# Two transformer layers on one core: gate values kept in SBUF for a batched gelu, DMA moves ordered by readiness with the broadcast split in four, paced block work, and two-bank score slots at the layer boundary

## The chip, the cores and the metric

The kernel runs on one core of one Trainium2 chip. The metric is the device time of one execution in microseconds (us). A quoted time is the median of several executions; a ratio is the mean time of one kernel's fast runs over the mean time of the other's fast runs of the same rounds, so it is not quite the ratio of the medians. Waits, busy times and stretches come from one profiled execution of each kernel, so a difference of spans need not equal that of the medians to the microsecond.

Five engines matter here. TensorE ("PE" in the profile, "PEld" for its weight loads) does all matrix products. ScalarE ("ACT") does exponentials and gelu. VectorE ("DVE") empties PSUM, does the statistics of the layer norms and takes over a part of the exponentials. GpSimd ("POOL") does a few products. The sync engine ("SP") only issues DMA.

## The reference, cut to what matters

One sequence of 2048 tokens, width 512, 32 heads of 16, a GEGLU hidden width of 1792. Two layers with the same weights:

```python
def _A_ref(x, wqkv, wo):                       # attention, 32 heads of 16
    qkv = (x @ wqkv).reshape(B, S, 3, H, Dh).transpose(2, 0, 3, 1, 4)
    q, k, v = qkv[0], qkv[1], qkv[2]
    scores = jnp.einsum("bhqd,bhkd->bhqk", q, k) * (Dh ** -0.5)
    p = jax.nn.softmax(scores, axis=-1)
    o = jnp.einsum("bhqk,bhkd->bhqd", p, v)
    return o.transpose(0, 2, 1, 3).reshape(B, S, D) @ wo

def _B_ref(x, w_gate, w_up, w_down):
    return (gelu_tanh(x @ w_gate) * (x @ w_up)) @ w_down

x = x + _A_ref(layernorm(x), wqkv, wo)
x = x + _B_ref(layernorm(x), w_gate, w_up, w_down)
x = x + _A_ref(layernorm(x), wqkv, wo)         # second layer, same weights
x = x + _B_ref(layernorm(x), w_gate, w_up, w_down)
```

## The kernel before

**A static order, made by a model.** The Python program does not loop over tiles in a fixed nest. It holds a small event model of the core, asks at each step which work is ready, emits that work, and advances the model's clock. What comes out is one fixed instruction order for each engine, with semaphores where data is passed on. So the durations in the model decide the *order*, the chip decides the *times*, and an engine that meets an instruction whose data is late stands until it is there, as PE does for 2.83 us in a view below.

**Attention.** A block is 512 queries. It has 8 units (4 heads each), and a unit has 64 score tiles of 128 keys by 512 queries. Score tiles are written by PE into a "slot" of up to three PSUM banks; there are two slots (banks 0 to 2 and 3 to 5). Bank 7 accumulates probabilities times V, bank 6 is the only spare bank. ScalarE exponentiates the tiles of a slot. In groups of 12 tiles (4 slots of 3), one tile of each slot can go to VectorE instead: it writes a rough exponential as integers, and three shifted copies that PE then multiplies too refine it. A VectorE group turns four three-bank exponentials into four two-bank ones.

```python
def vector_group():                    # may the next group of 12 use VectorE?
    if pend.get(("PI", dg_no[0] % NPI)):
        return False
    late = max(0.0, sch.free["dve"] - now[0]) + sum(op[3] for j in jobs["dve"] for op in j[2])
    late += 0.6 * len(shifts)
    return late < DVE_LATE

def a_slot(entry):
    layer, u, part, tiles, dslot, end = entry
    if dslot is not None:
        if dslot % 4 == 0:
            use["d"] = (layer or u) and vector_group()
        if not use["d"]:
            dslot = None
    ...
    na = n - (dslot is not None)       # tiles of this slot that ScalarE takes
    pe(fn, ...)                        # n score matmuls into the slot's banks
    o = sch.op("act", lambda e: e.activation(PT[...], PS[:, b0:b0 + na, :], ACTF.Exp, ...), ...)
```

**The post.** When a block's eight units are done, its "post" follows: normalise, output projection, residual, layer norm, gates, gelu, up, down, residual, layer norm. The post is a Python generator of PE pieces, and the pieces are put between the exponentials of the *next* block. That is what keeps ScalarE fed. At the boundary of the layers, the second layer starts with six units split in two parts, A (48 tiles) before the fourth post of the first layer is done and B after it.

Normalising sends the reciprocals of the softmax sums through a DRAM scratch and broadcasts them over partitions. GpSimd multiplies, and half of the products are moved by DMA from ATS into AT, the stationary operand of the output projection:

```python
def dma(eng, grp, dst, src, r=(), w=(), serial=False, kb=32):   # the model's price of a move
    t = max(sch.free[eng], sch.ready(eng, r, w)) + 0.5
    wire[0] = max(t, wire[0]) + kb / 180.0
    return sch.op(eng, ..., cost=0.5, lat=wire[0] - t + 1.7)

def spread():                                          # one unit's broadcast and product
    i, g = rest.pop(0)
    slot = rb_no[0] % NRB                              # NRB = 2 buffers
    dma("sp", "rb%d" % slot, RB[:, slot, :],
        AP(RSC, (half * 16 * HB + 16 * i) * 128, [[512, 4], [0, 32], [1, 512]]),
        r=[("RSC", half)], w=[("RB", slot)], serial=True, kb=256)
    ...
    def done(o):
        if odd:
            for j in range(4):
                dma("sp", "at%d_%d" % (c % 2, j), AT[32 * j + 16:32 * j + 32, c, :],
                    ATS[32 * j:32 * j + 16, c % 2, :], ...)
        ...
        spread()
    job("pool", 1, [(lambda e: e.tensor_tensor(dst, OS[:, os_, :], RB[:, slot, :], op=ALU.mult), ...)], done)
```

A DMA is issued at the point where the program asks for it, and SP works through its moves in that order. So a move whose data is late can hold back those behind it, the weight loads among them (two runs below show it: PE waits 19.4 us for down-projection weights with this order, in e8, and 2.5 us with moves ordered by readiness, in e5).

**Gates and gelu.** The gates of the post take over the two score slots. While they run there are no exponentials, only pairs of gate tiles and gelus from PSUM:

```python
def fill():
    if gq:
        return g_slot(*gq.pop(0))      # a pair of gate tiles instead of scores
    ...
def g_slot(qb, k):
    pe(fn, xk(qb) + [("WR", s)], bks, 8 * MM)           # 8 gate matmuls, two banks
    sch.op("act", lambda e: e.activation(HT[:, 2 * k:2 * k + 2, :], PS[:, b0:b0 + 2, :],
                                         ACTF.Gelu_apprx_tanh), ...)
```

**Where a piece of the post may go.** A piece is emitted when it fits into the time until ScalarE needs the next slot, with a tolerance. The tolerance grows when the post has fallen behind a count of slots; at the last block of a layer it is unlimited:

```python
def post_tol():
    if pace["haste"]:                  # the last post of a layer
        return 99.0
    return 1.0 if slot_no[0] > pace["start"] + 12 + 2.2 * pace["n"] else 0.1
```

If PE has nothing to do, the program emits dummy matmuls ("keep-clock" matmuls, the line with fONB and fZV) meant to keep TensorE's granted clock from dropping.

## Time and profile before

| | before |
|---|---|
| device time, median of 4 | 1822.8 us (1821.11 to 1826.94) |
| mean granted TensorE clock | 0.984 |
| exponentials on ScalarE | 1408 |
| score tiles on VectorE | 956 of 4096 |
| bytes moved by DMA | 126.14 MB |

The page's first part gives each engine's busy time, its share of the span, and its instructions.

```profile
span 1823.5 us, 39987 instructions
PE 1681.1 (92%) x17053; PEld 512.5 (28%) x17053; DVE 1410.7 (77%) x2322; ACT 1530.2 (84%) x1484; POOL 216.4 (12%) x237
```

PE looks like the limit, but 271.8 us of its time are keep-clock dummies. ScalarE has 293 us of idle time, and the question is what ended each idle stretch. This is ScalarE's list of waits before: what waited, for what, the us in total, how many times, and the longest one.

```profile
ACT fPT L1067 <- PE fPS L1062: 173.1, 104, 32.3
ACT fHT L1027 <- PE fPS L1021: 69.4, 49, 32.9
ACT fXNT L540 <- PE fPS L531: 17.5, 4, 15.6
```

Exponentials (fPT) wait 173.1 us for score matmuls, 32.3 us of it in one piece. Gelus (fHT) wait 69.4 us for gate matmuls; 32.9 us of that is a single wait in the tail, the rest is a steady drip, as ScalarE's timeline of one gelu phase before shows (start, duration, engine, line, operation, in brackets the idle time before it):

```profile
1407.48 1.02 ACT L1027 ACTIVATE fHT<-fPS 128x1024 bf16<-128x1024 f32 x1 [1.35 <-PE fPS L1021]
1409.20 1.02 ACT L1027 ACTIVATE fHT<-fPS 128x1024 bf16<-128x1024 f32 x1 [0.70 <-PE fPS L1021]
1410.93 1.02 ACT L1027 ACTIVATE fHT<-fPS 128x1024 bf16<-128x1024 f32 x1 [0.70 <-PE fPS L1021]
```

A pair of gates takes PE 1.73 us and a gelu 1.02 us, so ScalarE idles 0.7 us a pair. The table loads (1.28 us each, one before and one after the phase) come on top.

PE's own list of waits before has two lines that end in a DMA:

```profile
PE fPS L554 <- DMA fAT<-fATS: 16.8, 7, 3.2
PE fPS L858 <- DMA fWR<-in_B_w_down_dram: 14.1, 10, 5.2
```

The first is the output projection, standing for the copy of ATS into AT. What such a wait does is seen in the timeline of one post's start before:

```profile
1159.14 2.41 SPq L276 DMA_DIRECT2D fAT<-fATS  x4
...
1162.88 1.86 PE L554 MATMUL fPS<-fWO,fAT 128*128 128x512 bf16 x4 [2.83 <-DMA fAT<-fATS]
...
1164.67 1.03 PE L1062 MATMUL fPS<-fQ,fKT 32*128 32x512 bf16 x6
1165.33 1.94 ACT L1067 ACTIVATE fPT<-fPS 128x1024 bf16<-128x1024 f32 x2 [4.43 <-PE fPS L1062]
...
1166.04 1.05 PE L1172 MATMUL fPS<-fPP,fVD 128*17 128x512 f16 x4
...
1168.54 1.94 ACT L1067 ACTIVATE fPT<-fPS 128x1024 bf16<-128x1024 f32 x2 [1.28 <-PE fPS L1062]
...
1170.35 0.60 PE L1062 MATMUL fPS<-fQ,fKT 32*128 32x512 bf16 x6
```

PE stands 2.83 us. ScalarE then idles 4.43 us, and 1.28 us once more three microseconds later.

Why is the copy late? The chain of waits before passes through the broadcast of the reciprocals (start, duration, what):

```profile
463.86 7.04 DMA fRB<-rscr
...
1141.20 6.85 DMA fRB<-rscr
...
1152.39 5.30 DMA fRB<-rscr
```

The model allows 256/180 + 1.7 = 3.1 us for a lone 256 KB move. The broadcast took 5 to 7 us, with two under way. The DMA view of the kernel before, cut to the 7.5 us after 463.5, shows the busy share of the core's 16 DMA engines in tenths, and what they moved:

```profile
DMA  0000011112222222222222232252222222100002
GB/s 0 0 0 0 0 22 33 66 76 87 98 109 98 98 98 98 109 98 87 109 98 98 98 120 87 109 186 98 98 109 98 98 98 87 66 22 22 0 0 33
```

While nothing but broadcasts moves, "2" is two tenths and up to three of sixteen engines, hence 3.2 to 4.8 engines, at about 100 GB/s. The Trainium skill (DMA: Bandwidth & Descriptors, section "Why a DMA increments its semaphore by 16 and not by 1") says that a move uses the largest number of engines, at most 16, that divides the slowest dimension of both access patterns. The source of the broadcast is `[[512, 4], [0, 32], [1, 512]]`; its slowest dimension is 4, so four engines, and this trace agrees with that.

Last, ScalarE's timeline before at the layer boundary, the two longest idle stretches of the program outside its start and tail:

```profile
906.86 5.71 ACT L1067 ACTIVATE fPT<-fPS 128x1536 bf16<-128x1536 f32 x5 [32.31 <-PE fPS L1062]
...
1045.57 17.52 ACT L1067 ACTIVATE fPT<-fPS 128x1024 bf16<-128x1024 f32 x19 [28.62 <-PE fPS L1062]
```

### The profile page before, as it was taken

The numbers are of one execution on the slowest core, as the hardware profiler recorded it, in microseconds if no ns is written. First come the engines' busy times: TensorE is split into PE (matmuls) and PEld (weight loads), VectorE is DVE, ScalarE is ACT, GpSimd is POOL, SyncE is SP. The second block draws the span as 40 slices with busy tenths as digits, with TensorE's granted clock in tenths as the row PEclk, the third lists the DMA queues.
The fourth block names the chain that finished last, engine by engine and source line by source line (L and its number), as shares of the span: only waits on it lengthen the run. The fifth ranks groups of instructions, "written<-read, shape, count | busy, mean of one in ns | idle before, by whom it ended". The sixth has DMA issues, their size and how long they took to land.

```text
span 1823.5 us, 39987 instructions
## 1 busy us (share of the span) xinstructions
PE 1681.1 (92%) x17053; PEld 512.5 (28%) x17053; DVE 1410.7 (77%) x2322; ACT 1530.2 (84%) x1484; POOL 216.4 (12%) x237
## 2 busy tenths in 40 slices
PE   8998989999898998999899989899989999899998
PEld 3422223222232222322332322232223222232233
DVE  4798876889868878699568598769876988768853
ACT  2699998989889998899289389889998999889931
POOL 2402010011111021010331120101010010101010
PEclk9999999999999999999999999999999999999999
DMA  5200000152022410223312500023501152023403
GB/s 151 71 2 29 2 28 26 53 156 80 28 65 80 145 54 11 58 81 99 109 47 70 168 28 3 28 60 89 158 28 36 48 163 62 28 61 110 127 21 100
DMA packets 142775, 126.14 MB, mean 69 GB/s; under 512 B 8704, under 2 KB 126208, under 8 KB 142592
## 3 DMA queue, kind: packets, MB, share of 16 engines
q1 hardware_dynamic: 138320, 115.12, 21.1%
q0 software_dynamic: 4272, 8.39, 1.7%
q8 instruction: 139, 2.28, 0.5%
q14 instruction: 44, 0.36, 0.1%
HBM read 109.84 MB, written 6.82 MB: 64 GB/s over the span
## 4 chain that ended last, share of the span: by engine, by line
ACT 38%; PE 34%; DVE 12%; DMA 11%; SPq 2%; POOL 2%; issue 1%; POOLq 0%; DVEq 0%
ACT fPT L1067 37%; PE fPS L1062 7%; PE fPS L1172 7%; PE fPS L554 7%; PE fPS L1021 5%; DMA fRB<-rscr 5%; DVE fPI L1101 4%; PE fPS L1192 4%; DVE fPP L1123 3%; PE fPS L858 3%; DMA fWR<-in_B_w_down_dram 3%; SPq L276 2%; POOL fATS L745 1%; DVE fQ L596 1%; DMA rscr<-fLT 1%
## 5 line engine op out<-in xcount | busy, mean ns | idle before, releaser
L1067 ACT ACTIVATE fPT<-fPS 128x1024 bf16<-128x1024 f32 (+1 forms) x1408 | 1449.9, 1175 | 177.1 <-PE fPS L1062 173.1
L1101 DVE TENSOR_SCALAR fPI<-fPS 128x512 int16<-128x512 f32 x956 | 631.0, 686 | 222.3 <-PE fPS L1062 218.5
L1062 PE MATMUL fPS<-fQ,fKT 32*128 32x512 bf16 x4096 | 545.1, 388 | 69.4 <-ACT fPT L1067 51.4
L1123 DVE TENSOR_SCALAR fPP<-fPI 128x2048 int16<-128x2048 int16 x717 | 490.3, 722 | 7.1 <-PE fPS L1172 4.7
L1172 PE MATMUL fPS<-fPT,fVP 128*17 128x512 bf16 x3140 | 441.8, 387 | 8.7 <-DVE fOS L761 2.7
L1172 PE MATMUL fPS<-fPP,fVD 128*17 128x512 f16 x2868 | 374.9, 387 | 10.9 <-DVE fPP L1123 9.5
L1062 PEld LDWEIGHTS fPS<-fQ,fKT 32*128 32x128 bf16 x4096 | 136.5, 91 | 603.0 <-ACT fPT L1067 494.7
L1192 PE MATMUL fPS<-fONB,fZV 128*17 128x512 bf16 x3496 | 271.8, 387 | 5.2 <-POOL fONB L344 4.1
L1172 PE MATMUL fPS<-fPI,fVP 128*17 128x512 f16 x956 | 267.6, 388 | 2.5 <-DVE fPP L1123 2.5
L745 POOL TENSOR_TENSOR fAT<-fOS,fRB 128x512 bf16<-128x512 f32 x32 | 43.6, 1362 | 922.4 <-DMA fRB<-rscr 922.4
L1172 PEld LDWEIGHTS fPS<-fPT,fVP 128*17 128x17 f16 x3140 | 100.6, 88 | 159.5 <-issue 104.7
L858 PE MATMUL fPS<-fWR,fHT 128*128 128x512 bf16 x448 | 126.7, 386 | 14.4 <-DMA fWR<-in_B_w_down_dram 14.1
L1172 PEld LDWEIGHTS fPS<-fPP,fVD 128*17 128x17 f16 x2868 | 89.5, 89 | 121.6 <-issue 50.5
L554 PE MATMUL fPS<-fXNT,fWR 128*128 128x512 bf16 x448 | 113.9, 382 | 1.9 <-DVE fHT L844 1.5
L1027 ACT ACTIVATE fHT<-fPS 128x1024 bf16<-128x1024 f32 x56 | 57.3, 1023 | 69.5 <-PE fPS L1021 69.4
L844 DVE TENSOR_TENSOR fHT<-fPS,fHT 128x512 bf16<-128x512 f32 x112 | 76.8, 688 | 49.8 <-PE fPS L554 49.3
L1192 PEld LDWEIGHTS fPS<-fONB,fZV 128*17 128x17 f16 x3496 | 80.4, 91 | 80.7 <-issue 38.0
L1021 PE MATMUL fPS<-fXNT,fWR 128*128 128x512 bf16 x448 | 99.3, 380 | 0.9 <-ACT fPT L1067 0.7
L1172 PEld LDWEIGHTS fPS<-fPI,fVP 128*17 128x17 f16 x956 | 58.4, 88 | 49.6 <-issue 30.0
L629 POOL TENSOR_SCALAR fVD<-fVP 128x544 f16<-128x544 f16 (+1 forms) x48 | 53.2, 1110 | 154.1 <-DVE fVP L637 151.4
L1021 PEld LDWEIGHTS fPS<-fXNT,fWR 128*128 128x128 bf16 x448 | 42.6, 98 | 55.2 <-issue 3.1
L745 POOL TENSOR_TENSOR fATS<-fOS,fRB 128x512 bf16<-128x512 f32 x32 | 44.1, 1378 | 106.0 <-DMA fRB<-rscr 106.0
(58 smaller groups left out, 705.8 us busy)
## 6 DMA issues: line engine op xcount, KB each, us to landing
fWR<-in_B_w_down_dram SPq DMA_DIRECT2D x203, 256.0 KB, 3.2
fRB<-rscr SPq DMA_DIRECT2D x64, 256.0 KB
fWR<-in_B_w_gate_dram SPq DMA_DIRECT2D x56, 256.0 KB, 3.3
fWR<-in_B_w_up_dram SPq DMA_DIRECT2D x56, 256.0 KB, 2.9
fX<-in_A_x_dram POOLq DMA_DIRECT2D x7, 1024.0 KB, 5.7
xscr<-fX SPq DMA_DIRECT2D x16, 256.0 KB, 2.3
fX<-xscr SPq DMA_DIRECT2D x4, 1024.0 KB, 5.8
fAT<-fATS SPq DMA_DIRECT2D x128, 16.0 KB, 1.8
```

The lines of the kernel that those rows point to most:

```text
L554: ins = e.matmul(bank(bs[0])[:, 0:cols], lhsT=l, rhs=r_, start=(i == 0), stop=(i == n - 1))
L745: job("pool", 1, [(lambda e: e.tensor_tensor(dst, OS[:, os_, :], RB[:, slot, :], op=ALU.mult), [("OS", os_), ("RB", slot)], wk, 1.35)], done)
L844: (lambda e: e.tensor_tensor(HT[:, ft, :], bank(b), HT[:, ft, :], op=ALU.mult), [BK[b], ("HT", ft)], [("HT", ft)], 0.62)], got(("up", laye ...
L858: ins = e.matmul(bank(b)[:, 0:D], lhsT=HT[:, ft, i * 128:(i + 1) * 128], rhs=WR[:, s, jj * D:(jj + 1) * D], start=(ft == 0), stop=(ft == N ...
L1021: ins = e.matmul(bank(b0 + jj), lhsT=wchunk(s, jj, ck), rhs=XNT[:, ck, xs], start=(ck == 0), stop=(ck == NCK - 1))
L1027: sch.op("act", lambda e: e.activation(HT[:, 2 * k:2 * k + 2, :], PS[:, b0:b0 + 2, :], ACTF.Gelu_apprx_tanh), r=bks, w=[("HT", 2 * k), ("H ...
L1062: ins = e.matmul(bank(b0 + k), lhsT=KT[32 * j:32 * j + 32, c, kt * 128:(kt + 1) * 128], rhs=Q[32 * j:32 * j + 32, qs, :], start=True, stop ...
L1067: o = sch.op("act", lambda e: e.activation(PT[:, p, 0:512 * na].rearrange("p (a b) -> p a b", a=na), PS[:, b0:b0 + na, :], ACTF.Exp, scale ...
L1101: dve(0, [(lambda e: e.tensor_scalar(PI[:, gi, 512 * r:512 * (r + 1)], bank(b0 + n - 1), DBIAS, 0.0, op0=ALU.add, op1=ALU.max), [bks[-1]], ...
L1123: shifts.append((s, [(lambda e: e.tensor_scalar(PP[:, s, :], PI[:, gi, :], int(OCT) * ph // NPH, None, op0=ALU.add), [("PI", gi, r) for r ...
L1172: ins = e.matmul(PS[32 * j:32 * j + VW, ACC, :], lhsT=l, rhs=r_, start=a, stop=z, tile_position=(0, 32 * j), skip_group_check=True)
L1192: ins = e.matmul(PS[32 * j:32 * j + VW, ACC, :], lhsT=ZV[:, :], rhs=ones, start=False, stop=False, tile_position=(0, 32 * j), skip_group_c ...
```

## The change

It has five parts.

1. **Gate values in SBUF, one gelu batch a block.** Gates become pieces of the post like all others, placed between exponentials; VectorE copies them to SBUF, and when all 14 tiles are there two gelus of 3584 columns each run over them.
2. **Transfers by readiness.** SP gets a job list like VectorE and GpSimd: a move is put on the queue when the model says that its data is ready, and what depends on it waits in the model until it has been put there. The 256 KB broadcast becomes four moves of 32 KB (only the 16 partitions of each 32 that are used).
3. **Posts paced, VectorE tiles off when late.** A post has a schedule over its block; `behind()` is the number of pieces that it lags. Over 0 the tolerance grows, over `LAG` = 6 it is unlimited and no new VectorE group starts.
4. **Slots of two at the layer boundary.** While the last post of a layer runs (`haste`), slots have two tiles, all on ScalarE, and the third bank of each slot is lent to pieces of the post.
5. **Fewer weight passes.** At the last block of a layer the down projection does two token tiles a pass, so it reads its weights twice instead of four times.

A smaller part that the list leaves out: at the last block of a layer the layer norm's last step goes from GpSimd to VectorE.

The core of the diff:

```diff
 # 1: gates
-        gq.extend((qb, k) for k in range(NFT // 2))
+        for k in range(NFT // 2):
+            s = yield from wneed("g", k)
+            for jj in range(2):
+                ft = 2 * k + jj
+                def evac_g(b, ft=ft):
+                    if not tail:
+                        evac_job(1, b, [(lambda e: e.tensor_copy(HT[:, ft, :], bank(b)), [BK[b]], [("HT", ft)], 0.6)],
+                                 got(("gate", layer, qb, ft)))
+                        return
+                    ...                                 # the tail: gelu from PSUM, tile by tile
+                yield mm_piece([(wchunk(s, jj, ck), XNT[:, ck, xs]) for ck in range(NCK)], xk(qb) + [("WR", s)], evac_g)
...
+    def gelus(layer, qb):
+        for lo, hi in ((0, NFT // 2), (NFT // 2, NFT)):
+            keys = [("HT", i) for i in range(lo, hi)]
+            sch.op("act", lambda e, lo=lo, hi=hi: e.activation(HT[:, lo:hi, :], HT[:, lo:hi, :], ACTF.Gelu_apprx_tanh),
+                   r=keys, w=keys, cost=0.05 + 0.427 * (hi - lo) + (1.3 if not lo else 0), lat=0.16)
 # 2: moves
-    jobs = {"dve": [], "pool": []}
+    jobs = {"dve": [], "pool": [], "sp": []}
+    def move(prio, grp, dst, src, r, w, then=None, kb=32):
+        job("sp", prio, [(lambda: dma("sp", grp, dst, src, r=r, w=w, serial=True, kb=kb), r, w, None)], then)
...
-                dma("sp", "rb%d" % slot, RB[:, slot, :],
-                    AP(RSC, (half * 16 * HB + 16 * i) * 128, [[512, 4], [0, 32], [1, 512]]),
-                    r=[("RSC", half)], w=[("RB", slot)], serial=True, kb=256)
+            for j in range(4):
+                move(0, "rb%d_%d" % (slot, j), RB[32 * j:32 * j + 16, slot, :],
+                     AP(RSC, (half * 16 * HB + 16 * i + 4 * j) * 128, [[0, 16], [1, 512]]),
+                     [("RSC", half)], [("RB", slot, j)], landed)
 # 3: pace
+    def behind():
+        if not pace["on"]:
+            return 0.0
+        f = (tiles_filled[0] / (4.0 * NKT) - NG * (posts_done[0] + 1) - 1.0) / (NG - 1.5)
+        return PIECES * f - pace["n"]
     def post_tol():
-        if pace["haste"]:
+        if pace["haste"] or behind() > LAG:
             return 99.0
-        return 1.0 if slot_no[0] > pace["start"] + 12 + 2.2 * pace["n"] else 0.1
+        return 1.0 if behind() > 0 else 0.1
 # 3 and 4: the choice of slots
+            size = 3 if m is not None and not pace["haste"] else 2
+            d = size == 3 and (layer or u) and vector_group() and behind() < LAG
 # 4: banks for the post
+        if pace["haste"] and slot_no[0] >= 2 and not returned[0]:
+            pool_.update(3 * s + 2 for s in range(2) if not slot_open[s])
 # 5: weight passes
-        for ts in ([tts] if tail else [[tt] for tt in tts]):
+        for ts in ([tts] if tail else [tts[:2], tts[2:]] if qb == NQB - 1 and NQB > 1 else [[tt] for tt in tts]):
 ... (bookkeeping of held banks, weight waits, LT gathers and smaller model prices left out)
```

## The prediction

> **What bounds the kernel now.** ScalarE, and the places where it is starved. The page has it busy 1530.2 us of 1823.5 (84%): 1408 exponentials, 1449.9 us, and 57.3 us of gelu. The list of waits gives some 260 us of its idle time: 173.1 us of exponentials waiting for score matmuls, 69.4 us of gelu waiting for gate matmuls. PE (92%) contains 272 us of keep-clock dummies; VectorE is at 77%. The busy time by stretches shows ScalarE at 98% where it is fed (89.3 of 91 us, 1260 to 1351), 89% where a post starts (102.0 of 115 us, 1351 to 1466).
>
> Where ScalarE idles, from its timeline:
> 1. Layer boundary: 32.3 us before 906.9 (the third block's post ends late; a down-projection weight costs PE 5.2 us) and 28.6 us before 1045.6 (the fourth post works with one free PSUM bank).
> 2. Seven gelu phases: gates come every 1.73 us, gelus last 1.02 us, so 5.3 us idle each.
> 3. Start of six posts: 3 to 6 us (1165: 4.4+1.3). PE stands before the output projection for the copy of AT (16.8 us in total), because the 256 KB broadcast of reciprocals took 5 to 7 us in the chain, longer than the static order allowed for.
> 4. Tail: 73 us after the last exponential, a serial chain.
>
> **Change, costed.**
> - Gelu batch: removes 5.3 us idle and about 1 us of fixed cost per block (0.426 us per 512 columns, from the 1536 and 1024 exponentials, gives two calls of about 3.1 us). Table loads (1.28 us) stay. The Trainium skill (ScalarE: Activation LUTs, What ACT_TABLE_LOAD costs) has one price per element for every function; the trace agrees nearly (gelu 1023, exponential 1077 ns). Added: 14 VectorE copies a block, 98 x 0.69 = 67 us; at worst two VectorE groups a block are lost, each worth 4 x (1503-1077) = 1.7 us. Net gain 3 to 6 us a block.
> - Moves by readiness, broadcast halved and split in four: the output-projection stall mostly goes, 4 us x 6; weight waits (14.1 us on PE) shrink.
> - Pacing: the third post ends before its block; most of the 32 us goes.
> - Boundary: three banks for pieces shorten the fourth post. But slots of two, all on ScalarE, cost 0.54 us a tile instead of 0.35 on average (1450/4096): some 180 tiles x 0.19 = 34 us are paid back. The boundary (875 to 1046) shrinks from 171 to about 150 us, not by 61.
> - Tail: a faster broadcast, 2 us.
>
> Sum: 6 blocks x 7 = 42, boundary 21, tail 2, weight waits 3: about 66 us.
>
> **Prediction: 1757 us, 80% range 1725 to 1803.** Faster by over 2% (below 1787): 0.77; within 2%: 0.20; slower: 0.03.
>
> **What would show it right.** Gelu waits for gates gone but for the tail, 14 long gelu calls; PE waiting for AT under 5 us; the boundary's two long idle stretches under 20 us together; ScalarE share 87% or more; 880 to 940 VectorE tiles (956 now); more two-bank exponentials.
>
> **What would make it wrong.** Smaller gain: paced gate pieces of 0.86 us now fall between exponentials, and new waits for score matmuls eat the gelu gain; posts run late often, VectorE tiles are switched off widely and ScalarE's busy time grows by over 50 us; 256 quarter broadcasts of about 0.6 us issue clog the SP queue. Larger gain: the boundary idles vanish without the slots of two costing ScalarE.

## More of the kernel before

The busy time by stretches of the kernel before has the clock in a column (stretch, its length, then busy us and instructions of PE, PEld, DVE, ACT and POOL, then the granted clock, the DMA share and GB/s):

```profile
1163.00:1170.00 7.00, 7.00 (x43) 1.52 (x42) 3.34 (x6) 3.40 (x4) 0.00 (x0) 0.55 0.00 0
1170.00:1177.00 7.00, 6.64 (x75) 1.70 (x73) 6.27 (x12) 6.69 (x7) 0.00 (x0) 1.00 0.01 2
```

The Trainium skill (TensorE: Matmul & The Clock Gate, section "HAM oscillation — how this bites in real kernels") describes this pattern: PE waits for a DMA, the clock gate throttles, and the next burst of matmuls starts cold. This trace agrees, with 0.55 for seven microseconds.

## The result and the profile after

| | before | after |
|---|---|---|
| device time, median of 4 | 1822.8 us | 1768.23 us (1767.27 to 1771.39) |
| ratio of fast runs, 95% interval | | 0.970 (0.968 to 0.9721) |
| mean granted TensorE clock | 0.984 | 0.997 |
| exponentials, busy (sum of the two shapes) | 1473.3 us | 1543.8 us |
| score tiles on VectorE | 956 | 768 |
| bytes moved by DMA | 126.14 MB | 114.00 MB |

The kernel is 3.0% faster, about 55 us. One per cent of the kernel before is 18.2 us; the ratios below are turned into microseconds with that. The outputs agree with the reference.

First part of the page after:

```profile
span 1766.0 us, 38383 instructions
PE 1614.0 (91%) x16180; PEld 497.5 (28%) x16349; DVE 1276.4 (72%) x2103; ACT 1602.1 (91%) x1488; POOL 208.2 (12%) x226
```

ScalarE's busy time has *grown* by 72 us (1530.2 to 1602.1), and its idle time has fallen by 129 us (293.3 to 163.9). The net is the 57.5 us between the two spans. So the change did not take work away from ScalarE; it removed waits and paid with work. The instruction groups by shape show both sides (line, engine, operation, shapes, count, then busy us and mean ns of one, then idle time before). ScalarE before:

```profile
L1067 ACT ACTIVATE fPT<-fPS 128x1024 bf16<-128x1024 f32 x1084 | 1023.6, 1077 | 95.5 <-PE fPS L1062 92.3
L1067 ACT ACTIVATE fPT<-fPS 128x1536 bf16<-128x1536 f32 x324 | 449.7, 1503 | 81.6 <-PE fPS L1062 80.8
L1027 ACT ACTIVATE fHT<-fPS 128x1024 bf16<-128x1024 f32 x56 | 57.3, 1023 | 69.5 <-PE fPS L1021 69.4
```

and after:

```profile
L1128 ACT ACTIVATE fPT<-fPS 128x1024 bf16<-128x1024 f32 x992 | 932.4, 1078 | 43.2 <-PE fPS L1123 41.5
L1128 ACT ACTIVATE fPT<-fPS 128x1536 bf16<-128x1536 f32 x448 | 611.4, 1509 | 40.0 <-PE fPS L1123 39.5
L1094 ACT ACTIVATE fHT<-fHT 128x3584 bf16<-128x3584 bf16 x14 | 43.9, 3183 | 0.1
```

There are 124 more three-bank exponentials and 92 fewer two-bank ones: groups that were to go to VectorE went to ScalarE. Before, 239 of the 320 groups used VectorE (956 tiles, 4 a group); after, 192 did (768 tiles). Listing the decisions of the program that builds the order gives the reasons for the other 128: 68 because the post lagged, 9 because it lagged and VectorE was late as well, 30 because VectorE was late, 16 at the boundary with slots of two, 5 in the first unit. A group moved to ScalarE costs 4 x (1503 - 1077) ns = 1.7 us, so 47 groups should cost 80 us; the exponentials grew by 70.5.

ScalarE's list of waits after:

```profile
ACT fPT L1128 <- PE fPS L1123: 81.1, 75, 12.5
ACT L898 <- PE fPS L575: 30.1, 1, 30.1
ACT fXNT L561 <- PE fPS L552: 17.4, 3, 16.5
```

The wait for score matmuls fell from 173.1 to 81.1 us. The wait of gelus for gates is gone but for the tail (the 30.1 us on the table load there, 32.9 before). In PE's list of waits after, the output projection's wait for AT, 16.8 us before, is one wait of 0.8 us, and the wait for down-projection weights is gone:

```profile
PE fPS L575 <- DMA fAT<-fATS: 0.8, 1, 0.8
```

The DMA view after, over 6.5 us of the same phase as the one shown of before:

```profile
DMA  0000390790990320310410403900000004304109
GB/s 0 0 0 0 38 164 0 76 126 0 101 101 0 126 76 0 139 63 0 164 38 13 177 13 38 164 0 0 0 0 0 0 0 113 89 0 151 51 0 176
...
fRB<-rscr SPq DMA_DIRECT2D x12, 32.0 KB, 1.8
```

The engines are busy in short bursts, up to nine tenths of sixteen, and a quarter lands 1.8 us after its issue. The four quarters are issued one after another, so the whole gains less than a quarter does: from the first issue to the first product that needs it, it took 3.4 us here (456.81 to 460.19) and 5.1 us before (463.25 to 468.36); the medians over the kernel are 3.5 and 5.2 us. ScalarE's timeline after at the layer boundary:

```profile
877.90 10.12 ACT L1128 ACTIVATE fPT<-fPS 128x1536 bf16<-128x1536 f32 x10 [6.39 <-PE fPS L1123]
...
1044.76 26.05 ACT L1128 ACTIVATE fPT<-fPS 128x1024 bf16<-128x1024 f32 x26 [2.93 <-PE fPS L1123]
```

32.31 and 28.62 us have become 6.39 and 2.93.

**A table by stretches.** For each block GpSimd makes four products into AT and four into ATS, half of them before the block's last units are done, and the trace has the start of each. The start of the third product into AT is used as the mark of a block, the start of the last product into ATS as the mark of the tail. "Layer 1" is from the first block's mark to the fourth's, "boundary" from there to the fifth's, "layer 2" from there to the last ATS product, "tail" from there to the end of the span. All are from one profiled execution of each kernel. The experiments are in the table already; they are told below.

| kernel | to block 1 | layer 1 | boundary | layer 2 | tail | mean clock |
|---|---|---|---|---|---|---|
| before | 255.5 | 624.5 | 265.5 | 616.5 | 61.5 | 0.984 |
| after | 256.0 | 614.1 | 231.3 | 602.3 | 62.3 | 0.997 |
| before, broadcast split (e13) | 253.5 | 609.9 | 260.2 | 596.7 | 62.4 | 0.993 |
| after, both moves as before (e8) | 260.6 | 625.8 | 239.9 | 632.5 | 60.7 | 0.981 |
| after, moves at once (e3) | 258.9 | 610.9 | 233.4 | 608.0 | 60.5 | 0.993 |
| after, one broadcast (e5) | 257.4 | 617.3 | 239.2 | 610.2 | 60.1 | 0.989 |
| after, four moves of 64 KB (e11) | 259.6 | 613.7 | 233.9 | 603.7 | 60.1 | 0.996 |
| after, slots of three (e2) | 256.4 | 613.0 | 248.0 | 603.8 | 60.4 | 0.996 |
| after, gelu in pairs (e4) | 255.2 | 603.9 | 235.0 | 597.3 | 62.0 | 0.998 |
| gelu in pairs, LAG 12 (e10) | 256.1 | 604.6 | 236.7 | 588.5 | 60.8 | 0.996 |
| gelu in pairs, no switch (e14) | 254.9 | 602.5 | 262.4 | 596.3 | 63.6 | 0.995 |
| pacing alone (e7) | 264.0 | 630.5 | 268.1 | 617.9 | 59.3 | 0.976 |

The change gained 34.2 us at the boundary, 10.4 in layer 1, 14.2 in layer 2, and nothing in the tail. Most of the gain at the boundary does not come from the moves: with the moves of before (e8) it is still 25.6 us, and what e8 loses against the changed kernel it loses mainly in the layers (11.7 and 30.2 us).

### The profile page after: what moved, and what is told of

It is laid out like the page before. It is cut to its first block, busy times and chain, and to the rows that moved or that the text cites. A ratio compares the mean times of both kernels' runs of the same rounds, so it can differ in the third digit from the quotient of the medians.

```text
span 1766.0 us, 38383 instructions
## 1 busy us (share of the span) xinstructions
PE 1614.0 (91%) x16180; PEld 497.5 (28%) x16349; DVE 1276.4 (72%) x2103; ACT 1602.1 (91%) x1488; POOL 208.2 (12%) x226
## 2 busy tenths in 40 slices
DMA packets 138705, 114.00 MB, mean 65 GB/s; under 512 B 12320, under 2 KB 126240, under 8 KB 138528
## 4 chain that ended last, share of the span: by engine, by line
ACT 61%; PE 21%; DVE 14%; issue 1%; POOL 1%; DMA 1%; SPq 0%; DVEq 0%; POOLq 0%
ACT fPT L1128 58%; DVE fPI L1162 6%; PE fPS L575 6%; PE fPS L1123 5%; DVE fPP L1184 5%; PE fPS L1233 4%; PE fPS L1253 3%; ACT fHT L1094 2%; PE fPS L932 2%; DVE fQ L618 1%; PE fPS L638 1%; DVE fHT L545 1%; ACT L1094 1%; DMA fX<-in_A_x_dram 0%; POOL fVD L651 0%
## 5 line engine op out<-in xcount | busy, mean ns | idle before, releaser
L1128 ACT ACTIVATE fPT<-fPS 128x1024 bf16<-128x1024 f32 (+1 forms) x1440 | 1527.4, 1212 | 83.1 <-PE fPS L1123 81.1
L1162 DVE TENSOR_SCALAR fPI<-fPS 128x512 int16<-128x512 f32 x768 | 504.3, 683 | 65.5 <-PE fPS L1123 63.9
L1184 DVE TENSOR_SCALAR fPP<-fPI 128x2048 int16<-128x2048 int16 x576 | 393.7, 716 | 4.4 <-PE fPS L1233 3.4
L1123 PEld LDWEIGHTS fPS<-fQ,fKT 32*128 32x128 bf16 x4096 | 138.8, 91 | 617.3 <-ACT fPT L1128 527.1
L1233 PE MATMUL fPS<-fPP,fVD 128*17 128x512 f16 x2304 | 302.3, 381 | 6.4 <-DVE fPP L1184 6.1
L1253 PE MATMUL fPS<-fONB,fZV 128*17 128x512 bf16 x3356 | 256.6, 386 | 5.0 <-POOL fONB L344 4.1
L1233 PE MATMUL fPS<-fPI,fVP 128*17 128x512 f16 x768 | 217.4, 384 | 0.5 <-DVE fPP L1184 0.5
L895 DVE CAST fHT<-fPS 128x512 bf16<-128x512 f32 x98 | 67.5, 689 | 85.4 <-PE fPS L575 85.3
L575 PEld LDWEIGHTS fPS<-fXNT,fWR 128*128 128x128 bf16 x896 | 71.9, 97 | 123.2 <-DVE fHT L918 21.6
L1233 PEld LDWEIGHTS fPS<-fPP,fVD 128*17 128x17 f16 x2304 | 69.8, 88 | 88.8 <-issue 48.0
L808 DVE COPY fOS<-fPS 128x512 f32<-128x512 f32 x64 | 43.8, 684 | 23.8 <-PE fPS L1233 23.7
L1233 PEld LDWEIGHTS fPS<-fPI,fVP 128*17 128x17 f16 x768 | 47.4, 88 | 34.2 <-issue 19.3
## 6 DMA issues: line engine op xcount, KB each, us to landing
fWR<-in_B_w_down_dram SPq DMA_DIRECT2D x189, 256.0 KB, 3.0
fWR<-in_B_w_gate_dram SPq DMA_DIRECT2D x56, 256.0 KB, 3.3
fWR<-in_B_w_up_dram SPq DMA_DIRECT2D x56, 256.0 KB, 2.9
xscr<-fX SPq DMA_DIRECT2D x16, 256.0 KB, 2.1
```

The costliest lines, as they stand in the source:

```text
L575: ins = e.matmul(bank(bs[0])[:, 0:cols], lhsT=l, rhs=r_, start=(i == 0), stop=(i == n - 1))
L895: evac_job(1, b, [(lambda e: e.tensor_copy(HT[:, ft, :], bank(b)), [BK[b]], [("HT", ft)], 0.6)], got(("gate", layer, qb, ft)))
L1123: ins = e.matmul(bank(b0 + k), lhsT=KT[32 * j:32 * j + 32, c, kt * 128:(kt + 1) * 128], rhs=Q[32 * j:32 * j + 32, qs, :], start=True, stop ...
L1128: o = sch.op("act", lambda e: e.activation(PT[:, p, 0:512 * na].rearrange("p (a b) -> p a b", a=na), PS[:, b0:b0 + na, :], ACTF.Exp, scale ...
L1162: dve(0, [(lambda e: e.tensor_scalar(PI[:, gi, 512 * r:512 * (r + 1)], bank(b0 + n - 1), DBIAS, 0.0, op0=ALU.add, op1=ALU.max), [bks[-1]], ...
L1184: shifts.append((s, [(lambda e: e.tensor_scalar(PP[:, s, :], PI[:, gi, :], int(OCT) * ph // NPH, None, op0=ALU.add), [("PI", gi, r) for r ...
```

## The experiments

Three theories were put against each other. *Theory A* is the prediction's: gelu batch, moves and boundary each carry a share of similar size. *Theory B*: the broadcast and the clock that its lateness costs carry most of it. *Theory C*: the pacing and the switch carry it, since they keep posts inside their blocks. All twelve kernels ran with 3 rounds beside the kernel before. Each "expected" text was written before the run. Its theories A and B are those of that run, not these three.

### e1_ve_always: the VectorE switch taken out

```diff
-            d = size == 3 and (layer or u) and vector_group() and behind() < LAG
+            d = size == 3 and (layer or u) and vector_group()
```

> The changed kernel, but VectorE tiles are never switched off for a late post (68 groups of 12 tiles were switched off for that reason alone; 192 ran on VectorE, 239 before). Theory A, the switch earns its keep because PE has no room for the post's pieces beside four-matmul-heavy VectorE groups: slower than the changed kernel, 1780 to 1800 us (ratio to before 0.976 to 0.987); the third post ends late again and the boundary idles 15 us or more before layer 2. Theory B, the switch is a needless price (68 groups x 1.7 us = 116 us of ScalarE): faster than the changed kernel, below 1755 us (ratio under 0.963), ScalarE busy 1530 to 1560 us instead of 1602.

Measured: 1780.19 us, ratio 0.976 (0.9739 to 0.978), so 11 us slower than the change; and the result was **wrong**, with a relative error of 0.51. VectorE tiles rose to 976, and ScalarE was busy for 1518.3 us instead of 1602.1. The saving came back as waits: exponentials waited 148.7 us for scores (longest 55.6, at the boundary).

The order of instructions of this kernel shows why the result is wrong. The output projection of the third post comes after two products of the next block have been written into AT or ATS: in the trace ten products lie between the second projection and the third, which starts at 738.79, where the first two blocks have eight. No wait stands against that: the projection waits for AT to be *written*, and it has been, by the wrong block. In the listings of the other kernels the order is right, and they are correct. So the switch, which keeps the post from falling so far behind, is also a condition of correctness that no semaphore guards, and this run says nothing certain about time. The same question was asked again on a correct kernel in e14.

### e2_slots_of_three: the boundary's slots as before

```diff
-            size = 3 if m is not None and not pace["haste"] else 2
+            size = 3 if m is not None else 2
-        if pace["haste"] and slot_no[0] >= 2 and not returned[0]:
-            pool_.update(3 * s + 2 for s in range(2) if not slot_open[s])
```

> The changed kernel with slots of three tiles at the boundary too, and no slot bank lent to pieces there. Theory A, the extra two banks shorten the fourth post: slower by 20 to 35 us, 1788 to 1803 us (ratio 0.981 to 0.989), a ScalarE idle stretch of over 20 us before part B. Theory B, pacing alone mended the boundary and slots of two pay back what they earn: within 8 us of the changed kernel (ratio 0.966 to 0.974).

Measured: 1784.47 us, ratio 0.978 (0.976 to 0.98), correct. The slots of two, with the lent banks, are worth 0.8% or 15 us, less than theory A expected and more than theory B. In the table by stretches only the boundary moves, 231.3 to 248.0. An idle stretch of 30.1 us is back at the fourth post, and ScalarE is busy 15 us less (1587.3): that is what the slots of two cost, and their gain is net of it.

### e3_moves_at_once: no ordering by readiness, broadcast still split

```diff
 def move(prio, grp, dst, src, r, w, then=None, kb=32):
-    job("sp", prio, [(lambda: dma("sp", grp, dst, src, r=r, w=w, serial=True, kb=kb), r, w, None)], then)
+    o = dma("sp", grp, dst, src, r=r, w=w, serial=True, kb=kb)
+    if then is not None:
+        then(o)
 # and the same for the weight loads
```

> The changed kernel with every move put on the SP queue when the program asks for it, not when its data is ready; the quartered broadcast stays. Theory A, order by readiness took the PE stalls on AT and on weights away: slower by 10 to 25 us, 1778 to 1793 us (ratio 0.975 to 0.984), PE waits for fAT 10 us or more and for weights about 10. Theory B, the quartered broadcast did it: within 6 us of the changed kernel, PE waits for fAT under 4 us.

Measured: 1770.21 us, ratio 0.9696 (0.9675 to 0.9716), correct; the changed kernel had 0.970, so theory B held. As long as the broadcast is split, the order by readiness, a good part of the diff, is worth nothing that can be measured.

### e4_gelu_pairs: gates in the score slots and gelus in pairs, as before

```diff
+    def g_slot(qb, k):                       # as in the kernel before; counts two pieces for the pace
+        take_slot()
+        pace["n"] += 2
+        ...
+        sch.op("act", lambda e: e.activation(HT[:, 2 * k:2 * k + 2, :], PS[:, b0:b0 + 2, :], ACTF.Gelu_apprx_tanh), ...)
-                    evac_job(1, b, [(lambda e: e.tensor_copy(HT[:, ft, :], bank(b)), ...
-            gelu_q.append((layer, qb))
 # all else as changed
```

> The changed kernel with the gates of before: computed in the score slots, gelu of two tiles each straight from PSUM, no VectorE copies; all else as changed. Theory A, the batch is worth its idle time (7 x 5.3 us, less lost VectorE groups): slower by 15 to 35 us, 1783 to 1803 us (ratio 0.978 to 0.989), with gelu waiting about 35 us plus the tail. Theory B, the 98 copies and the pieces between exponentials eat it: within 8 us of the changed kernel (ratio 0.966 to 0.974).

Measured: 1761.59 us, ratio 0.9655 (0.9635 to 0.9674), correct. Undoing the gelu batch made the kernel 0.45% or about 8 us *faster*. The two intervals do not quite touch (0.9674 here, 0.968 there), so the sign is likely and the size uncertain; a gain of the size predicted for the batch is ruled out. Theory A fell.

Where does it come from? Compare one gelu phase in both, first ScalarE's and PE's busy time by stretches in the changed kernel (columns as above):

```profile
1344.00:1386.00 42.00, 39.12 (x349) 12.00 (x351) 24.48 (x40) 41.72 (x37) 2.97 (x4) 1.00 0.14 39
1386.97:1395.82 8.85, 7.56 (x106) 2.97 (x106) 2.10 (x3) 8.83 (x4) 0.00 (x0) 1.00 0.04 12
```

and then in the kernel with gelus in pairs:

```profile
1341.92:1355.90 13.98, 13.40 (x70) 5.45 (x70) 0.69 (x1) 9.73 (x10) 0.00 (x0) 1.00 0.46 131
```

The batch makes the phase 5.1 us shorter (8.85 against 13.98), as predicted, and ScalarE is full in it. But PE is not: of its 7.56 us, 5.10 are keep-clock dummies. With pairs, PE is busy for 13.40 us, and 11.07 of those are gate matmuls, useful work done while ScalarE works on gelu. With the batch, those 11 us must be found beforehand, between exponentials, where PE is already full: in the 42 us before the phase it is busy for 39.12 us, and only 2.86 of these are dummies (with pairs, the 41.9 us before the phase hold 7.76 us of dummies). The post lags, the switch takes groups from VectorE (24.48 of 42 us busy), and ScalarE gets them. VectorE groups: 192 with the batch, 224 with pairs. ScalarE's exponentials: 1543.8 against 1490.8 us by shape, 53 us, which is 32 x 1.7. What the batch saves in waits, ScalarE pays in work. The listing of the program's decisions names the reason: without the batch 32 groups were off for a lagging post alone, with it 68, while those off for a late VectorE alone are not more but fewer with the batch (30 against 43).

### e9_pairs_plus_copies: e4 with the copies' VectorE load added

One rival reading of e4 was that the 98 gate copies (67.5 us of VectorE) made VectorE late, which turns groups off. So e4 was given 98 useless VectorE instructions of about the same length, two beside each pair of gates, with the order of PE and ScalarE unchanged:

```diff
 def g_slot(qb, k):
+    for _ in range(2):
+        dve(1, [(lambda e: e.bn_stats(DUS[:, :], WO[:, 0:2, :].bitcast(F32)...), [("WO",)], [("DUS",)], 0.6)])
```

> The run with gelu in pairs (ratio 0.9655) plus 98 VectorE statistics over a constant tile (about 0.69 us each, 67 us, result unused), two beside each pair: the VectorE load of the copies without their place on PE. The order on PE and ScalarE is the same as in that run. Theory A, the batch loses because it parts ScalarE's gelu from PE's gates, so that PE idles in one and is short in the other: VectorE load costs little, ratio 0.964 to 0.968. Theory B, the batch loses by the 98 copies on VectorE: back to the changed kernel, ratio 0.969 or more.

Measured: 1759.05 us, ratio 0.9636 (0.962 to 0.9652), correct: not slower than e4, if anything a little faster, so theory B of this run fell. But these instructions do not stand where the copies of the change stand. VectorE's timeline of this kernel shows 14 of them in one piece at the start of a gelu phase, where VectorE had little else to do, and the other six phases are the same:

```profile
1343.14 10.16 DVE L1105 BATCH_NORM_STATS2 fDUS<-fWO 128x6 f32<-128x512 f32 x14
```

The copies of the change lie between exponentials. So e9 shows that 68 us more of VectorE work are free in the gelu phases, and says nothing certain of copies elsewhere. Against an overloaded VectorE speak the listing in e4 and the 24.48 of 42 us for which VectorE is busy before the phase; the copies are not quite free in the program's model, though. With their price set to nothing there, the scheduling code of the changed kernel gives 203 groups instead of 192, where pairs have 224 (no kernel was run with that). So the loss of overlap between PE's gates and ScalarE's gelus is the larger part as far as the order shows, and a part of up to about 11 of the 32 groups may be the copies.

### e7_pacing_alone: the kernel before with the pacing and the switch only

```diff
 # built from e4, with these undone:
-            size = 3 if m is not None and not pace["haste"] else 2
+            size = 3 if m is not None else 2
 # moves at once as in e3; one 256 KB broadcast; four down passes at the boundary; no bank lent
```

> The kernel before with only the pacing taken from the change (progress counted in tiles, any tolerance and no VectorE tiles when more than 6 pieces behind); gelu in pairs from PSUM, moves at once, one 256 KB broadcast, slots of three and four passes of down weights at the boundary. Theory A, pacing takes the first boundary idle (32 us) away by itself, and the second (28 us) and the AT stalls stay: 1785 to 1803 us (ratio 0.979 to 0.989), two idle stretches at the boundary of under 12 and over 20 us, PE waits for fAT over 10 us. Theory B, pacing needs the other parts to be worth anything, its lost VectorE tiles cost as much as the idle: ratio 0.99 or more.

Measured: 1834.47 us, ratio 1.0048 (1.0032 to 1.0065), correct: a small *loss*, as this run's theory B expected. The kernel is not quite the kernel before with one part more: it keeps the tail, the layer norm on VectorE and the bookkeeping of the change. With that said, theory C falls. The third post now ends in its block (the 32.3 us idle before 906.9 has become 2.22), but the fourth post, alone in its place with one spare bank, waits longer. ScalarE's timeline of this kernel at the boundary:

```profile
897.80 8.29 ACT L1151 ACTIVATE fPT<-fPS 128x1536 bf16<-128x1536 f32 x8 [2.22 <-PE fPS L1146]
...
1062.09 8.44 ACT L1151 ACTIVATE fPT<-fPS 128x1024 bf16<-128x1024 f32 x9 [46.76 <-PE fPS L1146]
```

The idle time moved from the first gap to the second (32.3 + 28.6 before, 2.2 + 46.8 here), and the clock was at its lowest of all kernels, 0.976 in the profiled execution.

### e8_moves_of_before: the changed kernel with the moves of the kernel before

```diff
 # e3 (moves at once), and
-            for j in range(4):
-                move(0, "rb%d_%d" % (slot, j), RB[32 * j:32 * j + 16, slot, :],
-                     AP(RSC, (half * 16 * HB + 16 * i + 4 * j) * 128, [[0, 16], [1, 512]]), ...)
+            move(0, "rb%d" % slot, RB[:, slot, :],
+                 AP(RSC, (half * 16 * HB + 16 * i) * 128, [[512, 4], [0, 32], [1, 512]]), ..., kb=256)
```

> The changed kernel with both parts of the moves undone: at once instead of by readiness, and one 256 KB broadcast instead of four of 32 KB. The run with only the order undone was as fast as the change. Theory A, the quartered broadcast is what took the AT stall away: PE waits for fAT back to 10 us or more, 1778 to 1790 us (ratio 0.975 to 0.982). Theory B, the paced post hides the longer broadcast: within 6 us of the changed kernel (ratio 0.967 to 0.973).

Measured: 1818.39 us, ratio 0.9949 (0.9923 to 0.9976), correct. Both theories of the run expected less of a loss. Without its moves the change is worth half a per cent. The moves are worth 2.5%, some 45 us, of a total of 55. First part of its page, then its ScalarE list of waits, then PE's:

```profile
PE 1639.2 (90%) x16287; PEld 500.5 (28%) x16461; DVE 1279.5 (70%) x2110; ACT 1602.5 (88%) x1490; POOL 206.9 (11%) x226
```

```profile
ACT fPT L1128 <- PE fPS L1123: 134.1, 96, 15.3
```

```profile
PE fPS L932 <- DMA fWR<-in_B_w_down_dram: 19.4, 7, 4.9
...
PE fPS L577 <- DMA fAT<-fATS: 9.7, 5, 4.1
```

This is the cleanest pair. ScalarE is busy for 1602.5 us here and 1602.1 us in the changed kernel, so its work is nearly the same (the static order is not, as the model prices the moves differently: 772 tiles on VectorE instead of 768); its wait for score matmuls differs, 134.1 against 81.1 us, and that is the 53 us between the two spans. PE itself stood for DMA for 29 us here, and for 0.8 us there. The clock differs too: 0.981 here, 0.997 there. As an estimate, (1 - clock) x span is 35 us of lost full-speed PE time here and 5 us in the changed kernel.

### e5_one_broadcast: order by readiness kept, broadcast not split

```diff
 # as in e8, but moves still go by readiness
```

> The changed kernel with one 256 KB broadcast a unit instead of four of 32 KB; order by readiness stays. Undoing the order alone cost nothing (ratio 0.9696), undoing both cost 46 us (0.9949). Theory A, the quartered broadcast alone carries the gain of the moves: ratio 0.988 to 0.996, PE waits for fAT about 10 us. Theory B, either one is enough: ratio 0.968 to 0.975.

Measured: 1786.08 us, ratio 0.9791 (0.9765 to 0.9816), correct. Splitting is worth 0.9% or 17 us where moves go by readiness (e5 to the changed kernel) and 2.5% where they don't (e8 to e3). PE waits 14.6 us for AT here and only 2.5 us for weights. Both theories missed: the ratio lies between them. So order by readiness does something, 1.6% or 29 us from e8 to e5, but only in the presence of slow broadcasts: PE's wait for weights falls from 19.4 us to 2.5. Splitting makes it unnecessary.

### e11_four_of_64k: spread over engines or fewer bytes?

The split quarter is 32 KB, since it also leaves out the 16 partitions of each 32 that nobody reads. Here the four moves carry all 256 KB:

```diff
 # e3, and
-                move(0, ..., RB[32 * j:32 * j + 16, slot, :], AP(RSC, ..., [[0, 16], [1, 512]]), ...)
+                move(0, ..., RB[32 * j:32 * j + 32, slot, :], AP(RSC, ..., [[0, 32], [1, 512]]), ...)
```

> The run with moves at once, with the quartered broadcast at its old size: four moves of 64 KB, to all 32 partitions of each quarter. The trace of before has about 2 tenths of the 16 DMA engines busy, at about 101 GB/s, for as long as a broadcast runs. Theory A, the one move ran on 4 of 16 engines and four moves with a slowest dimension of 32 run on all: halving the bytes matters little, ratio 0.968 to 0.974. Theory B, the bytes matter: ratio 0.98 or more.

Measured: 1774.36 us, ratio 0.9724 (0.97 to 0.9748), correct. Theory A held. Against e3 (0.9696), with the same static order, the second half of the bytes costs 0.3%, with intervals that overlap; against e8 (0.9949), with as many bytes in one move, it gains 2.2%. The median from issue to landing was 2.0 us for 64 KB and 1.8 us for 32 KB. From the first issue to the first product it took 3.5 us here (460.70 to 464.21; the median is 3.6). The gain does not come from the bytes but from splitting the move. How much of it is the number of engines and how much the static order, which the model's price of the move changes as well, these runs do not part. Whether one move of 128 KB with an outermost dimension of 4 would do worse or better was not run, and stays open.

### e13_before_quartered: the split broadcast alone, on the kernel before

```diff
 # the kernel before, and
-                dma("sp", "rb%d" % slot, RB[:, slot, :],
-                    AP(RSC, (half * 16 * HB + 16 * i) * 128, [[512, 4], [0, 32], [1, 512]]),
-                    r=[("RSC", half)], w=[("RB", slot)], serial=True, kb=256)
+                for j in range(4):
+                    dma("sp", "rb%d_%d" % (slot, j), RB[32 * j:32 * j + 16, slot, :],
+                        AP(RSC, (half * 16 * HB + 16 * i + 4 * j) * 128, [[0, 16], [1, 512]]),
+                        r=[("RSC", half)], w=[("RB", slot, j)], serial=True)
 # and RB zeroed once at the start
```

> The kernel before with nothing but the quartered broadcast. Theory A, it is most of the change's gain whatever stands around it: 1775 to 1800 us (ratio 0.973 to 0.987), PE waits for fAT under 6 us instead of 16.8. Theory B, it pays only together with the pacing, which ties the rest of the block to the post's start: 1803 to 1822 us (ratio 0.988 to 0.999).

Measured: 1785.51 us, ratio 0.978 (0.9755 to 0.9805), correct. Theory A held. A handful of changed lines bring 40 of the change's 55 us. In the table by stretches the gain is in the layers (14.6 and 19.8 us) and hardly at the boundary (5.3 us). At the boundary the first long idle stretch is gone, but the second grew from 28.62 us, as ScalarE's timeline of this kernel shows:

```profile
1024.89 17.61 ACT L1069 ACTIVATE fPT<-fPS 128x1024 bf16<-128x1024 f32 x19 [37.88 <-PE fPS L1064]
```

VectorE tiles even rise (968), ScalarE's busy time falls a little (1522.5). No wait of PE for AT is left in its list, and the clock is 0.993. Note that the split also changes the model's price of the broadcast, and so the static order; the run cannot part the two. An obvious rival was not run either: the one broadcast left as it is, with an honest price in the model (5 to 7 us instead of 3.1), so that the order no longer puts the projection before its data.

### e14_pairs_always: e1 asked again, on a kernel that is right

```diff
 # e4, and
-            d = size == 3 and (layer or u) and vector_group() and behind() < LAG
+            d = size == 3 and (layer or u) and vector_group()
```

> The run with gelu in pairs with VectorE tiles never switched off for a late post: 249 groups on VectorE, 224 at a lag of 6 (ratio 0.9655) and 237 at a lag of 12 (0.9587). In the instruction order no post falls so far behind that the buffer AT is overwritten, so the result should be correct, other than in the run without the switch on the changed kernel. Theory A, once gates are out of the pieces the switch is only a price: below 1747 us (ratio under 0.957). Theory B, without it PE falls behind at the layer boundary: over 1755 us (ratio over 0.962), with a boundary idle stretch of 15 us or more.

Measured: 1781.13 us, ratio 0.9758 (0.9732 to 0.9785), correct; 1.0% or 19 us slower than e4, as theory B expected. ScalarE is busy for only 1513.8 us, 41 less than in e4. The saving comes back at the boundary, in ScalarE's timeline of this kernel:

```profile
893.08 1.02 ACT L1155 ACTIVATE fPT<-fPS 128x1024 bf16<-128x1024 f32 x1 [40.19 <-PE fPS L1150]
```

By stretches, layers 1 and 2 gain 1.4 and 1.0 us over e4, and the boundary loses 27.4. The switch is needed, but for the boundary alone.

### e10_pairs_lag12: the best of what the runs pointed to

If the switch is needed only to have posts done by the boundary, a looser threshold should keep that and lose fewer groups:

```diff
 # e4, and
-    LAG = 6
+    LAG = 12
```

> The run with gelu in pairs, and VectorE tiles switched off only when the post is more than 12 pieces behind instead of 6: 237 groups on VectorE instead of 224 (192 in the changed kernel). Theory A, each group is worth 1.7 us of ScalarE and PE now has room: 13 x 1.7 = 22 us faster at most, 1740 to 1757 us (ratio 0.955 to 0.962). Theory B, PE is short and gives the gain back in waits for score matmuls: within 5 us of the run with pairs (ratio 0.963 to 0.968).

Measured: 1749.79 us, ratio 0.9587 (0.9566 to 0.9609), correct. Theory A held. It is the fastest kernel here, 4.1% faster than the kernel before, and faster than the change by 18 us by the medians or 1.1% of the kernel before by the ratios. VectorE takes 237 groups (948 tiles), ScalarE is busy for 1533.2 us; the boundary stays at 236.7 us and layer 2 shrinks to 588.5. This threshold was tried with pairs only; with the batch it was not run.

## Why the prediction was right or wrong

The total was right: 1757 us predicted, 1768.23 measured, inside the range, and faster by over 2%. Its terms were not. That the total was near is in part luck: the gelu term was too high by about 26 us (18 predicted, -8 measured), the moves and the boundary too low by some 18 and 13.

- **What bounds the kernel: right.** ScalarE and the places where it starves. Busy time grew by 72 us and the kernel still gained, because the waits fell by 129 us.
- **"Gelu batch ... Net gain 3 to 6 us a block": wrong, in all likelihood sign included.** The sum used the lower end, 6 x 3 = 18 us (7 a block less 4 for the stall); undoing the batch gained about 8 us (e4). The step that failed was to count the 5.3 us of ScalarE idle time as free and the gates as costing only VectorE copies. The idle time was the price of an overlap: PE did 11 us of gates there. Moved between exponentials, they push the post behind, and ScalarE gets back VectorE's groups (32 x 1.7 = 54 us; measured 53). The VectorE copies, the cost that the prediction did name, are the smaller part at most (e9 and the listing of decisions); that part is not shown by a run.
- **"The output-projection stall mostly goes, 4 us x 6; weight waits (14.1 us on PE) shrink": right in mechanism, too small.** The sum of 24 + 3 us was predicted; 45 us were measured by undoing the moves (e8) and 40 by adding the split alone (e13). The prediction counted ScalarE's idle time at six starts and does not name the clock: after a stall of 2.83 us the granted clock was 0.55 for 7 us, and half clock came ten times between start and tail, not six. Kernels with unsplit broadcasts ran at 0.976 to 0.989, those with split ones at 0.993 to 0.998. That the clock carries the rest is an estimate from these numbers; no run changed the clock alone. That PE's wait for AT would fall under 5 us was right (0.8), and the risk that 256 broadcasts would clog SP's queue did not come true as far as PE's waits show.
- **"Moves by readiness": no part of the gain as the change stands.** The prediction did not part the order from the split. e3 does: 0.9696 without the order, 0.970 with it.
- **"The boundary (875 to 1046) shrinks from 171 to about 150 us": right in direction, too small.** It shrank by 34 us by the marks of the table, between which lie 265.5 us and not 171. The idle stretches predicted under 20 us together were 6.39 + 2.93. The cost of the slots of two, put at 34 us, was about 15 us by ScalarE's busy time (e2), and their net gain 15 us. Pacing alone, which was to give "most of the 32 us", only moved the idle time to the next gap (e7): 2.2 + 46.8 us. It needs the slots of two behind it.
- **"Tail: a faster broadcast, 2 us": wrong, no effect.** 61.5 us before, 62.3 after. The broadcast is not what the tail waits for.
- **"880 to 940 VectorE tiles", "more two-bank exponentials": wrong.** 768 tiles; 992 two-bank exponentials instead of 1084. This is what the prediction listed under what would make it wrong ("VectorE tiles are switched off widely and ScalarE's busy time grows by over 50 us"): it happened, with 72 us. The total still held because the moves (45 against 27 us) and the boundary (34 against 21) gave more than was counted, though these parts overlap and do not add up to the 55 us. "ScalarE share 87% or more" (91%) and 14 long gelu calls were right.

What stays open: the order of instructions is the outcome of a model, and any small edit shuffles it. What such a shuffle is worth was not measured. e4 and e9 have the same order on PE and ScalarE and yet differ by 0.2%, about 3.5 us, with e9, which has more work, the faster: that is the size of what the comparison cannot resolve. So effects under some 5 us in this document should not be trusted, and the 8 us of the gelu batch stand on e4's tile counts as much as on its time. Not shown either: the clock apart from the late moves, the split apart from its price in the model, part 5 and the layer norm on VectorE by themselves. The parts also do not add up: e7 loses 9 us where e8, which also has the slots of two, the lent banks, the gelu batch and fewer weight passes, gains 9.

## What to carry to other kernels

When an engine is starved at the start of a phase, look for the late DMA first and at the shape of its access pattern: a broadcast whose outermost dimension is 4 kept some four of sixteen engines busy, and writing it as four moves with an outermost dimension of 16 (with the order that came of it) gave 40 of 55 us for a few lines. Idle time of the limiting engine may be the visible side of an overlap with another full engine: before removing it, ask where that engine's work will go and what is displaced there. And where a static order is paced by a threshold, undo each part on its own and tune the threshold afterwards: the best kernel here keeps four of the change's five parts, drops one, and doubles one number.

## What the Trainium skill lacked or had wrong

- *DMA: Bandwidth & Descriptors.* The rule that the slowest dimension sets the number of engines held, and it should have a time beside it. The 256 KB broadcast with an outermost dimension of 4 ran at about 100 GB/s on some 4 of 16 engines and took 5 to 7 us with two under way. As four moves with an outermost dimension of 32, each quarter landed 2.0 us after its issue (e11), and quarters of 32 KB after 1.8 us; from the first issue to the first product that made medians of 3.6 and 3.5 us, against 5.2. For the kernel this was 2.2 to 2.5%, the change of order included.
- *DMA: Bandwidth & Descriptors, section "Rules for kernel authors".* "Coalesce into one large transfer; under 64 KB you're paying mostly overhead" pointed the wrong way here: four moves of 32 KB beat one of 256 KB (0.978 against 1, e13; half of the bytes were left out too, which e3 and e11 put at 0.3%). The row "Use all 16 engines" of the same table holds the reason; the two should refer to each other, since coalescing is what made the outermost dimension 4.
- *TensorE: Matmul & The Clock Gate, section "HAM oscillation — how this bites in real kernels".* It gives about 3.4 us as the idle gap that brings the clock down. Here the records show a gap of 2.83 us on PE, after which the clock was 0.55 for 7 us; it also has no example of what that costs an engine fed by PE (ScalarE idled 4.43 + 1.28 us for the 2.83 us).
- *ScalarE: Activation LUTs, section "What ACT_TABLE_LOAD costs".* The load of 1283 ns and the price of an activation agree (186 + 0.833 x 3584 = 3172 ns by the page, 3183 measured). The drain of about 1380 ns for each switch is not seen: an exponential of 1.53 us began at 1385.42, the load began at 1386.97, and the gelu at 1388.27, so this switch cost 1.3 us.
